# Windowed attention with sinks and a two-product block on one core: two of the first product's tiles move to the values' banks in the last attention stage, and the last block of outputs goes out in parts

## The chip, the cores and the metric

The kernel runs on one core of one Trainium2 chip. The metric is the device time of one execution in microseconds (us). Three executions of the kernel before took 249.0, 248.71 and 250.2 us; their median is 249.0 us.

## The reference: what is computed

Four sequences of 768 tokens with 8 heads of width 64 go through attention in which a query sees the first four keys (the sinks) and the 128 keys up to its own. The result, 3072 rows of 512, goes through two products with a gate between them.

```python
keep = is_sink | in_window            # pos < 4, or 0 <= query - key < 128
scores = np.where(keep, scale * np.matmul(q, k.transpose(0, 1, 3, 2)), -1000000000.0)
a = np.exp(scores - np.max(scores, axis=-1, keepdims=True))
a = a / (np.sum(a, axis=-1, keepdims=True) + 1e-09)
attn_out = np.matmul(a, v)

h = x @ w_in                          # x: 3072 x 512, w_in: 512 x 2048
g = h * (1.0 / (1.0 + np.exp(-1.702 * h)))
return (g @ w_out).astype(np.float32) # w_out: 2048 x 512
```

## The kernel before

**Tiling.** The tokens are cut into NG = 12 groups of 256, three to a sequence. A group has two row blocks of 128 tokens (called i) and four pairs of heads (called hp).

**Attention of a group.** `scores` multiplies queries and keys into a PSUM tile of two banks (tag "nat"). `maxima` (VectorE, L230 to L243) merges the keys of two blocks and takes the maxima. `weights` (ScalarE, L251) takes exponentials. `weights_transposed` (L270) turns them with a transposing DMA on SyncE's queue. `lower` (VectorE, L300) and `upper` (GpSimd, L313) cut them to the window's two triangles, and `values` (L319 to L341, TensorE) multiplies them with the values into a bank of tag "av". `normal` (L356 and L357, VectorE) divides by the sums and so gives that bank free. `x_transposed` (L375) turns the group's result with one transposing DMA on SyncE's queue.

**The two products of a group.** `hidden(g, F2)` (L379 to L394) computes one eighth of the first product: eight matmuls of 256 columns into one bank of tag "mm", and one gate activation on ScalarE (L390) that reads the bank into gT. `out_part` (L396 to L402) is the second product: for each row block 16 matmuls of 512 columns, all into one bank of tag "mm". `out_store` (L404 to L412) copies that bank to a tile osb, on ScalarE for row block 0 (L408) and on VectorE for row block 1 (L410), and stores its 256 KB with one DMA on SyncE's queue (L412).

**Banks.** PSUM has 8 banks. The tag "nat" holds two tiles of two banks, "mm" two banks (L103 to L104), and "av" two banks (L106 to L107). A tag's banks are taken in turn: the tile after next waits until the first one's readers are done. In the tag "av", `sink_transposed` (L288 to L293, one matmul and a VectorE copy L292) takes a bank before the four tiles of `values`.

**Order.** The schedule is manual: each engine and queue works in the order in which the program writes the instructions. The main loop (from L520) runs n from 1 to 13. In pass n the attention of group n, the first product of group n - 1 (g1) and the second product of group n - 2 (g2) are woven together. A pass first writes the exponentials and the second product, and then a loop over F2 from 0 to 7 (from L571), in which `hidden(g1, F2)` comes first, then `sink_transposed` at F2 = 1, the next group's `scores` at F2 = 1, and the four `values` tiles at the steps listed in a tuple (L590).

**The last passes.** In pass 11 the last attention group (11) runs beside the first product of group 10; there are no scores of a next group. Pass 12 has the second product of group 10 and then the first of group 11. Pass 13 has only the second product of group 11, 32 matmuls, and its two stores. ScalarE needs one function table for the exponentials and another for the gate, so that in every pass it loads a table before the first gate (ACT_TABLE_LOAD, L390) and before the first exponential (L251). The copy on ScalarE needs none of its own.

Of the kernel before, what the change touches and what calls it, by code (L numbers as in the profile page):

```python
# [10 lines left out]
FP32 = mybir.dt.float32  # L11
# [6 lines left out]
P = 128  # L18
D = 64
TG = 256  # L20
# [37 lines left out]
def kernel(  # L58
# [11 lines left out]
    nc = tc.nc  # L70
    B, H, S, Dh = q.shape
    n_sink, window = int(n_sink), int(window)
    assert (B, H, S, Dh) == (4, 8, 768, D) and n_sink == 4 and window == P
    DM = H * Dh
    DF = moe_w_in.shape[1]
    HP = H // 2
    NF = DF // P
    NT = S // TG
    NG = B * NT
# [5 lines left out]
    work = ctx.enter_context(tc.tile_pool(name="work", bufs=2))  # L85
# [4 lines left out]
    w_out16 = big.tile([P, NF, DM], FP16, name="w_out16")  # L90
# [12 lines left out]
    def mm_bank(name, shape=(P, 512), dt=FP32):  # L103
        return psp.tile(list(shape), dt, tag="mm", bufs=2, name=name)  # L104
# [4 lines left out]
    G = [dict() for _ in range(NG)]  # L109
# [57 lines left out]
    def sink_keys(b: int, copy):  # L167
        kT = G[b * NT]["qkT"]
        for h in range(2):
            copy(  # L170
                out=kd[b][bass.ts(h, D), :, bass.ts(h, n_sink)],
                in_=kT[bass.ts(h, D), 1, 0, :, 0:n_sink],
            )
# [49 lines left out]
    def kinds(mask, t: int):  # L223

        m = mask.rearrange("p (i c) -> p i c", i=2)
        if t == 0:
            return m.unsqueeze(1).broadcast_to((P, 2, 2, P))
        return m[:, 1:2].unsqueeze(1).broadcast_to((P, 2, 2, P))

    def maxima(g: int, hp: int):  # L230
        nat = G[g]["nat", hp]
        nc.vector.copy_predicated(  # L232
            out=nat[:, :, :, P:], mask=kinds(take_prev, g % NT), data=nat[:, :, :, 0:P]
        )
        m1 = work.tile([P, 2, 2], FP32, tag="m1", name=f"m1{g}_{hp}")
        nc.vector.tensor_reduce(  # L236
            out=m1.rearrange("p h i -> p (h i)"), in_=nat.rearrange("p h i c -> p (h i) c")[:, :, P:],
            axis=AX.X, op=ALU.max,
        )
        nc.vector.scalar_tensor_tensor(  # L240
            out=G[g]["bias"][:, :, hp], in0=m1.rearrange("p h i -> p i h"), scalar=-scale,
            in1=G[g]["m2"][:, :, hp], op0=ALU.mult, op1=ALU.min,
        )  # L243

    def weights(g: int, hp: int):

        nat, bias = G[g]["nat", hp], G[g]["bias"]
        A = work.tile([P, 4, P], FP16, tag="A", bufs=4, name=f"A{g}_{hp}")
        for h in range(2):
            for i in range(2):  # L250
                nc.scalar.activation(  # L251
                    out=A[:, 2 * h + i], in_=nat[:, h, i, P:], func=AF.Exp, bias=bias[:, i, hp, h : h + 1],
                    scale=scale,
                )
        G[g]["A", hp] = A

    def weights_transposed(g: int, hp: int):
        A = G[g]["A", hp]
        AT = work.tile([P, 2, 2, P], FP16, tag="AT", bufs=6, name=f"AT{g}_{hp}")
        flat = AT.rearrange("p h i s -> p (h i) s")  # L260
        if g < 2:
            tp = mm_bank(f"tA{g}_{hp}", (P, 4, P), FP16)
            for a in range(4):
                nc.tensor.transpose(tp[:, a], A[:, a], ident)  # L264
            if g == 0 or hp < 3:
                nc.scalar.copy(flat, tp)
            else:
                nc.vector.tensor_copy(out=flat, in_=tp)
        else:
            nc.sync.dma_start_transpose(flat, A.rearrange("p a c -> p (a c)"))  # L270
        G[g]["AT", hp] = AT
# [10 lines left out]
    def sink_weights(g: int):  # L282
        ts_ = G[g]["ts"]
        As = sinkA[g % 2]
        nc.scalar.activation(out=As[:, 0:64], in_=ts_.rearrange("p a j -> p (a j)"), func=AF.Exp)
        G[g]["As"] = As
# [92 lines left out]
    def hidden(g: int, F2: int):  # L379
        xT = G[g]["xT"]  # L380
        if F2 == 0:
            G[g]["gT"] = work.tile([P, NF, TG], FP16, tag="gT", bufs=3, name=f"gT{g}")
        hT = mm_bank(f"hT{g}_{F2}", (P, 2, 2, P))
        for f in range(2):
            F = 2 * F2 + f
            for c in range(4):
                nc.tensor.matmul(  # L387
                    hT[:, f], w_in16[:, c, bass.ts(F, P)], xT[:, :, c], start=(c == 0), stop=(c == 3)
                )
        nc.scalar.activation(  # L390
            out=G[g]["gT"][:, 2 * F2 : 2 * F2 + 2].rearrange("p f s -> p (f s)"),
            in_=hT.rearrange("p f i s -> p (f i s)"),
            func=AF.Gelu_apprx_sigmoid,
        )  # L394

    def out_part(g: int, i: int, part: int):  # L396

        if part == 0:
            G[g]["o", i] = mm_bank(f"o{g}_{i}")
        o, gT = G[g]["o", i], G[g]["gT"]  # L400
        for F in range(4 * part, 4 * part + 4):
            nc.tensor.matmul(o, gT[:, F, bass.ts(i, P)], w_out16[:, F], start=(F == 0), stop=(F == NF - 1))  # L402

    def out_store(g: int, i: int):  # L404
        b, t = divmod(g, NT)
        osb = work.tile([P, DM], FP32, tag="osb", bufs=3, name=f"osb{g}_{i}")
        if i == 0:
            nc.scalar.copy(osb, G[g]["o", i])  # L408
        else:
            nc.vector.tensor_copy(out=osb, in_=G[g]["o", i])  # L410
        r = b * S + t * TG + i * P
        nc.sync.dma_start(out[r : r + P, :], osb)  # L412
# [44 lines left out]
    def o(g: int, i: int, *parts):  # L457
        if 0 <= g < NG:
            for p in parts:
                out_part(g, i, p)  # L460
# [59 lines left out]
    for n in range(1, NG + LAG2):  # L520
        att, first = n < NG, n == 1
        g1, g2 = n - LAG1, n - LAG2
        if att and n + 1 < NG and (n + 1) % NT == 0:
            sink_keys((n + 1) // NT, nc.gpsimd.tensor_copy)

        if first:
            sink_weights(1)
        else:
            if att:
                for hp in (0, 1):  # L530
                    weights(n, hp)
                    weights_transposed(n, hp)
            o(g2, 0, 0, 1, 2, 3)
            if att:
                scores(n, 2)
                maxima(n, 2)
            o(g2, 1, 0)
            if att:
                scores(n, 3)
                maxima(n, 3)  # L540
                sink_terms(n)
            o(g2, 1, 1, 2, 3)
            out_store(g2, 0)
            if att:
                weights(n, 2)
                weights_transposed(n, 2)
            out_store(g2, 1)
            if att:
                weights(n, 3)
                weights_transposed(n, 3)  # L550
                sink_weights(n)
                lower(n, 0)
                if n + 2 < NG:
                    transposed_qk(n + 2)
        if att:
            upper(n, 0)
            upper(n, 1)
            if first:
                upper(n, 2)
                upper(n, 3)  # L560
                load_v(3)
                load_qk(4)
                load_v(4)
            else:
                for part in range(4):
                    if n + 3 < NG:
                        load_part(n + 3, part)
                    if part < 2:
                        upper(n, 2 + part)

        for F2 in range(NF // 2):  # L571
            if 0 <= g1 < NG:
                hidden(g1, F2)
            if not att:
                continue
            if F2 == 1:
                sink_transposed(n)
                if first:
                    lower(n, 0)
            if first and F2 in (2, 3):  # L580
                transposed_qk(2, (F2 - 2,))
            if F2 == (6 if first else 1):
                ahead(n + 1, 0)
            if F2 == 1:
                lower(n, 1)
            if F2 == (7 if first else 1):
                ahead(n + 1, 1)
            if F2 == 2:
                lower(n, 2)
            for hp, at in enumerate((4, 5, 6, 7) if first else (3, 4, 6, 7)):  # L590
                if F2 == at:
                    values(n, hp)
                    if hp == 0:
                        lower(n, 3)
                    normal(n, hp)
                    if not first and hp in (1, 2):
                        paced_load(n + 3, 3 + hp, n, hp)
        if att:
            x_transposed(n)
            if n + 1 < NG and (n + 1) % NT == 0:  # L600
                sink_values((n + 1) // NT)
            if first:
                transposed_qk(3)
# [34 lines left out]
```

## Time and profile before

| | |
|---|---|
| median of three executions | 249.0 us |
| the profiled execution's own time | 249.51 us |
| its span, first to last instruction | 247.8 us |
| mean granted TensorE clock | 0.966 |
| TensorE busy | 222.1 us, 90% of the span |
| ScalarE busy | 154.3 us, 62% |
| VectorE busy | 148.0 us, 60% |
| share of TensorE in the chain that ended last | 63% |

The span is 1.7 us shorter than the execution's own time, and that execution is 0.5 us above the median. In the profile, PE is TensorE's matmul, PEld its weight load, DVE VectorE, ACT ScalarE, POOL GpSimd and SP SyncE; a q behind an engine is its queue. "L387" is line 387 of the kernel. A row of the timeline gives start, duration, engine, line, operation and count, and in brackets the engine's idle time before it and what ended that. A row of the chain of waits gives start, duration, engine and what it did. The view of DMA traffic cuts a window into 40 slices and gives the rate in each.

### The profile page before, as it was taken

What the parts mean: (1) busy time and instruction counts of PE and PEld (TensorE: products, weight loads), DVE (VectorE), ACT (ScalarE), POOL (GpSimd) and SP (SyncE); (2) the same over time, 40 slices, a digit from 0 to 9 for tenths busy, and PEclk for the clock granted to TensorE, in tenths of its full rate; (3) what the DMA queues carried; (4) which work ended last, traced back from release to release, by engine and by line L of the source; (5) the groups of instructions that cost most, each with busy time, mean ns of one, the idle gap of its engine ahead of it and who ended that gap; (6) DMA issues with size and microseconds to landing.
All of it is one profiled execution on the core that took longest, in us unless ns stands there. A gap on an engine that the chain in (4) does not pass through costs nothing.

```text
span 247.8 us, 5720 instructions
## 1 busy us (share of the span) xinstructions
PE 222.1 (90%) x2172; PEld 151.8 (61%) x2172; DVE 148.0 (60%) x390; ACT 154.3 (62%) x350; POOL 99.9 (40%) x152
## 2 busy tenths in 40 slices
PE   0654779699999999999999999999999999799993
PEld 0542559548748649558478477487485694594851
DVE  7679725847757478379577467586682783730101
ACT  2286476277667775875775776677668757751430
POOL 8988594407622616637235276156110210310000
PEclk9996559999999999999999999999999999999999
DMA  9999999999999999999989989999992513503102
GB/s 81 152 197 198 163 207 182 154 127 174 178 146 131 158 169 142 130 202 160 129 165 122 163 150 159 160 144 143 157 157 43 139 33 68 147 3 85 42 3 86
DMA packets 134668, 33.13 MB, mean 134 GB/s; under 512 B 127344, under 2 KB 131568, under 8 KB 134640
## 3 DMA queue, kind: packets, MB, share of 16 engines
q0 software_dynamic: 79104, 13.64, 72.6%
q1 hardware_dynamic: 55104, 18.99, 43.8%
q8 instruction: 17, 0.28, 0.5%
q10 hardware_dynamic: 432, 0.13, 0.2%
q14 instruction: 11, 0.09, 0.1%
HBM read 27.50 MB, written 6.29 MB: 136 GB/s over the span
## 4 chain that ended last, share of the span: by engine, by line
PE 63%; DMA 13%; DVE 10%; ACT 8%; issue 3%; SPq 2%; ACTq 0%; DVEq 0%
PE hT L387 30%; PE o L402 20%; DMA xT<-xn 9%; ACT A L251 4%; DVE m L236 3%; DVE nat L232 3%; PE nat L220 2%; DMA AT<-A 2%; PE av L339 2%; ACT L390 2%; PE av L327 2%; PE av L335 2%; PE tA L264 2%; DMA vsr<-in_v_dram 2%; SPq L424 1%
## 5 line engine op out<-in xcount | busy, mean ns | idle before, releaser
L387 PE MATMUL hT<-xT,w_in 128*128 128x256 f16 x768 | 95.5, 275 | 3.2 <-ACT gT L390 1.7
L402 PE MATMUL o<-w_out,gT 128*128 128x512 f16 x384 | 88.3, 380 | 0.0
L387 PEld LDWEIGHTS <-w_in 128*128 128x128 f16 x768 | 72.9, 99 | 16.4 <-DMA xT<-xn 2.6
L390 ACT ACTIVATE gT<-hT 128x512 f16<-128x512 f32 x96 | 56.2, 597 | 42.3 <-PE hT L387 42.2
L251 ACT ACTIVATE A<-nat,bias 128x128 f16<-128x128 f32 x192 | 53.8, 376 | 26.2 <-DVE bias L240 23.0
L313 POOL TENSOR_SCALAR_AFFINE_SELECT up<-AT 128x512 f16<-128x512 f16 (+1 forms) x48 | 28.0, 594 | 92.0 <-DMA AT<-A 86.8
L402 PEld LDWEIGHTS <-gT 128*128 128x128 f16 x384 | 35.2, 98 | 39.9
L232 DVE COPY_PREDICATED nat<-prev,nat 128x512 f32<-128x512 uint16 x48 | 33.2, 692 | 30.0 <-ACT A L251 13.1
L236 DVE TENSOR_REDUCE m<-nat 128x4 f32<-128x512 f32 x48 | 33.2, 691 | 1.6
L123 POOL DMA_DIRECT2D qkn<-in_q_dram x24 | 21.6, 910 | 5.0 <-DMA w_out<-in_moe_w_out_dram 3.3
L410 DVE COPY osb<-o 128x512 f32<-128x512 f32 x12 | 8.3, 690 | 23.7 <-PE o L402 23.7
L123 POOL DMA_DIRECT2D qkn<-in_k_dram x24 | 21.3, 895 | 1.9 <-DMA w_in<-in_moe_w_in_dram 1.6
L123 POOL DMA_DIRECT2D vn<-in_v_dram x24 | 21.3, 895 | 1.6 <-issue 1.1
L357 DVE TENSOR_TENSOR xn<-av,rcp 128x256 f16<-128x256 f32 x48 | 20.4, 424 | 1.7
L300 DVE TENSOR_TENSOR lo<-AT,own 128x512 f16<-128x512 f16 (+1 forms) x48 | 18.9, 413 | 2.1 <-DMA AT<-A 2.1
L335 PE MATMUL av<-vn,up 128*128 128x65 f16 x160 | 18.3, 195 | 0.0
L339 PE MATMUL av<-vn,lo 128*128 128x65 f16 x160 | 18.3, 196 | 0.0
L356 DVE RECIPROCAL rcp<-av 128x4 f32<-128x4 f32 x48 | 8.6, 179 | 14.6 <-PE av L339 14.4
L220 PEld LDWEIGHTS <-qkT 64*128 64x128 f16 x352 | 11.5, 99 | 8.5 <-issue 8.1
L327 PE MATMUL av<-vs,AsT 128*128 128x130 f16 x80 | 16.5, 224 | 0.0
L220 PE MATMUL nat<-qkT 64*128 64x128 f16 x288 | 16.0, 228 | 0.0
L335 PEld LDWEIGHTS <-up 128*128 128x128 f16 x160 | 14.8, 100 | 0.6 <-issue 0.2
(51 smaller groups left out, 168.2 us busy)
## 6 DMA issues: line engine op xcount, KB each, us to landing
out_dram<-osb SPq DMA_DIRECT2D x24, 256.0 KB
qkn<-in_q_dram POOLq DMA_DIRECT2D x24, 128.0 KB, 5.3
qkn<-in_k_dram POOLq DMA_DIRECT2D x24, 128.0 KB, 5.0
vn<-in_v_dram POOLq DMA_DIRECT2D x24, 128.0 KB, 5.5
w_in<-in_moe_w_in_dram POOLq DMA_DIRECT2D x4, 512.0 KB, 9.1
w_out<-in_moe_w_out_dram POOLq DMA_DIRECT2D x4, 512.0 KB, 10.6
AT<-A SPq DMA_TRANSPOSE x40
xT<-xn SPq DMA_TRANSPOSE x10
```

Source lines behind the costliest of these rows:

```text
L123: nc.gpsimd.dma_start(dst, (q, k, v)[e][b, :, rows].rearrange("h s d -> s h d"))
L220: nc.tensor.matmul(o, qkT[r, 0, i, hp], keys[r], start=True, stop=True)
L232: nc.vector.copy_predicated(out=nat[:, :, :, P:], mask=kinds(take_prev, g % NT), data=nat[:, :, :, 0:P])
L236: nc.vector.tensor_reduce(out=m1.rearrange("p h i -> p (h i)"), in_=nat.rearrange("p h i c -> p (h i) c")[:, :, P:], axis=AX.X, op=ALU.max,)
L251: nc.scalar.activation(out=A[:, 2 * h + i], in_=nat[:, h, i, P:], func=AF.Exp, bias=bias[:, i, hp, h : h + 1], scale=scale,)
L313: nc.gpsimd.affine_select(out=out, in_=in_, pattern=[[0, rows], [-1, P]], compare_op=ALU.is_gt, fill=zero_reg, base=0, channel_multiplier=1,)
L327: nc.tensor.matmul(av[:, i].rearrange("p h d -> p (h d)"), AsT, vs[b][:, c : c + 2].rearrange("p h d -> p (h d)"), start=True, stop=False,)
L335: nc.tensor.matmul(av[:, i, h], up[:, h, i], vn[b][J // 2][:, J % 2, head], start=False, stop=False)
L339: nc.tensor.matmul(av[:, i, h], own_w[:, h, i], vn[b][t][:, i, head], start=(I == 0), stop=(I == 0 or h == 1))
L387: nc.tensor.matmul(hT[:, f], w_in16[:, c, bass.ts(F, P)], xT[:, :, c], start=(c == 0), stop=(c == 3))
L390: nc.scalar.activation(out=G[g]["gT"][:, 2 * F2 : 2 * F2 + 2].rearrange("p f s -> p (f s)"), in_=hT.rearrange("p f i s -> p (f i s)"), fun ...
L402: nc.tensor.matmul(o, gT[:, F, bass.ts(i, P)], w_out16[:, F], start=(F == 0), stop=(F == NF - 1))
```

## The change

1. In pass 11, `hidden(10, 2)` and `hidden(10, 3)` take their bank from the tag "av" and not from "mm".
2. In the same pass the four `values` tiles are written at F2 = 4, 5, 6, 7 and not at 3, 4, 6, 7.
3. In pass 13, the store of row block 0 is written directly behind its product. Row block 1 goes through a new function `out_last`: its 512 columns are made in two halves of 256, each with 16 matmuls into a bank of "mm" of its own. The first half is copied by ScalarE and stored by one DMA on SyncE's queue (128 KB). Of the second half, VectorE copies the first 128 columns, stored on SyncE's queue, and ScalarE copies the last 128 columns, stored on ScalarE's own queue (64 KB each).

```diff
@@ hidden
-        hT = mm_bank(f"hT{g}_{F2}", (P, 2, 2, P))
+        bank = av_bank if g == NG - 2 and F2 in (2, 3) else mm_bank
+        hT = bank(f"hT{g}_{F2}", (P, 2, 2, P))
@@ new function
+    def out_last(g: int, i: int):
+        b, t = divmod(g, NT)
+        gT, r = G[g]["gT"], b * S + t * TG + i * P
+        osb = work.tile([P, DM], FP32, tag="osb", bufs=3, name=f"osb{g}_{i}")
+        for half in range(2):
+            c = bass.ts(half, DM // 2)
+            o = mm_bank(f"o{g}_{i}_{half}", (P, DM // 2))
+            for F in range(NF):
+                nc.tensor.matmul(o, gT[:, F, bass.ts(i, P)], w_out16[:, F, c], start=(F == 0), stop=(F == NF - 1))
+            if half == 0:
+                nc.scalar.copy(osb[:, c], o)
+                nc.sync.dma_start(out[r : r + P, c], osb[:, c])
+            else:
+                d, a = bass.ts(2, P), bass.ts(3, P)
+                nc.vector.tensor_copy(out=osb[:, d], in_=o[:, 0:P])
+                nc.sync.dma_start(out[r : r + P, d], osb[:, d])
+                nc.scalar.copy(osb[:, a], o[:, P:])
+                nc.scalar.dma_start(out[r : r + P, a], osb[:, a])
@@ main loop, pass n
+            if g2 == NG - 1:
+                out_store(g2, 0)
+                out_last(g2, 1)
+                continue
             o(g2, 1, 0)
@@ loop over F2
-            for hp, at in enumerate((4, 5, 6, 7) if first else (3, 4, 6, 7)):
+            for hp, at in enumerate((4, 5, 6, 7) if first else (3, 4, 6, 7) if n + 1 < NG else (4, 5, 6, 7)):
```

## The prediction

> **What bounds the kernel now.** I read the page first, then the waits of TensorE in the last passes, the chain of waits and the timeline of the passes that the change touches. The page:
>
> ```profile
> span 247.8 us, 5720 instructions
> PE 222.1 (90%) x2172; PEld 151.8 (61%) x2172; DVE 148.0 (60%) x390; ACT 154.3 (62%) x350; POOL 99.9 (40%) x152
> ```
>
> TensorE is the bound on average, so a change pays where TensorE stands still, or behind its last matmul. TensorE's waits from 205 to 224 us have one row, and the table by stage shows its place:
>
> ```profile
> PE hT L387 <- ACT gT L390: 1.4, 1, 1.4
> ...
> 214.90:216.32 1.42, 0.00 (x1) 0.00 (x1) 1.32 (x3) 1.41 (x3) 0.74 (x1) 1.00 0.89 259
> 216.32:223.14 6.82, 6.82 (x89) 6.20 (x89) 2.25 (x7) 3.74 (x7) 0.80 (x1) 1.00 0.03 6
> ```
>
> The third column is TensorE's busy time: nothing for 1.42 us in pass 11, and then 6.82 of 6.82 us, at full clock (1.00). Why it stops is in the timeline:
>
> ```profile
> 214.08 0.27 ACT L285 ACTIVATE sinkA<-ts 128x64 f16<-128x64 f32 x1
> 214.37 1.28 ACT L390 ACT_TABLE_LOAD   x1
> ...
> 214.68 0.22 PE L290 MATMUL tAs<-ident,sinkA 128*128 128x128 f16 x1
> 214.94 0.23 DVE L292 COPY AsT<-tAs 128x128 f16<-128x128 f16 x1 [0.85 <-PE tAs L290]
> ...
> 215.67 1.08 ACT L390 ACTIVATE gT<-hT 128x512 f16<-128x512 f32 x2
> 216.32 1.91 PE L387 MATMUL hT<-xT,w_in 128*128 128x256 f16 x16 [1.42 <-ACT gT L390]
> ```
>
> The first two tiles of the first product fill both "mm" banks. ScalarE still has exponentials to do and then a table to load, so that its first gate runs from 215.67 to 216.28 (0.60 us, two of them in 1.08: one each 0.48). The third tile needs the first one's bank. It needs nothing else: its other inputs served the tiles ahead of it.
>
> The rest of the span is TensorE without a gap, and then the tail:
>
> ```profile
> 230.04 7.11 PE hT L387 x64
> 237.16 6.92 PE o L402 x32
> 244.08 0.03 DVEq L410
> 244.11 0.04 issue
> 244.16 0.69 DVE osb L410
> ...
> 244.87 0.33 SPq L412 DMA_DIRECT2D out_dram<-osb  x1
> GB/s 0 0 0 0 0 0 0 0 0 0 0 0 0 0 0 0 0 348 389 369 369 348 410 328 62 0 0 0 0 0 0 0 0 0 0 0 0 0 0 0
> ...
> L633 SPq DRAIN  x3: 7/7/13, 247.0 to 247.3; - x3
> ```
>
> The row of rates is the DMA traffic of 244 to 248 us in slices of 0.1; the last row is the queue's first step behind its wait for the store. From the last matmul (244.08) to the end of the span (247.8) are 3.72 us: 0.08 until VectorE starts, 0.69 for its copy, 0.02 until the store is issued, 0.8 until bytes move (245.7), 0.75 for 256 KB, and 1.38 for the notice (0.55, to 247.0) and the closing barrier.
>
> **Step 1: two tiles in the "av" banks.** The order of "av" banks is: fourth values tile of group 10, the sinks' transpose of pass 11, hT 2, hT 3, then values 0 to 3. hT 2 follows a bank whose reader was group 10's last VectorE division, in pass 10; it is free. TensorE can go on behind the transpose, which streams 128 columns from 214.68, at about 214.74. The chain has the unit costs:
>
> ```profile
> 216.32 1.91 PE hT L387 x16
> 218.22 0.06 PE av L327
> ...
> 218.58 0.87 PE hT L387 x8
> ...
> 219.81 1.75 PE hT L387 x16
> 221.55 0.06 PE av L327
> ...
> 221.91 0.87 PE hT L387 x8
> ```
>
> A tile of hT is 0.87 us and a tile of values 0.36 (218.22 to 218.58). The new order then runs: hT 2 to 215.61; hT 3, whose bank is that of the transpose, free when VectorE's copy ends at 215.17, to 216.48; hT 4, in the "mm" bank that the first gate frees at 216.28, to 217.35; values 0 to 217.71, in the bank of hT 2, which the third gate frees at 215.67 + 2 x 0.48 + 0.60 = 217.23; hT 5 (second gate ends at 216.75) to 218.58; values 1 (fourth gate: 217.71) to 218.94; hT 6, values 2, hT 7 and values 3 at 219.81, 220.17, 221.04 and 221.40. Each bank is free before it is wanted; the smallest margins are 0.12 us (values 0) and 0.20 (hT 4). So the gain lies between 1.42, the idle time, and 1.58, which adds the 0.16 that the first sixteen matmuls behind the gap took longer (1.91 against 1.75). I take 1.5.
>
> Step 2, values one F2 later, costs nothing by itself: the four tiles stay in order, the last remains behind hT 7, and the triangles are ready:
>
> ```profile
> 217.04 0.43 DVE L300 TENSOR_TENSOR lo<-AT,own 128x512 f16<-128x512 f16 x1 [0.78 <-DMA AT<-A]
> 217.16 0.80 POOL L313 TENSOR_SCALAR_AFFINE_SELECT up<-AT 128x512 f16<-128x512 f16 x1 [1.18 <-DMA AT<-A]
> ...
> 223.85 1.23 SPq L375 DMA_TRANSPOSE xT<-xn  x1
> ...
> DMA  0000000000699999700000000599700000000000
> ```
>
> The fourth triangles are there at 217.96 and wanted at 221.04. On VectorE, the division for values 0 stays behind `lower` of the fourth pair; that ends at 217.47, and values 0 at 217.71. Without this step, values 0 would stand ahead of hT 4, and wait for the third gate from 216.48 to 217.23. On SyncE's queue nothing is moved past anything, and GpSimd has no loads left. Behind pass 11, the turned xT of group 11 is needed when the second product of group 10 ends; its DMA moved from 225.0 to 226.4 (last row, slices of 0.2 from 223), over 3 us ahead of 230.04. It starts as much earlier as TensorE does, so the margin stays.
>
> **Step 3: the second product in halves.** 32 matmuls of 256 columns replace 16 of 512. The chain gives 6.92 / 32 = 0.216 for 512 columns, and for 256 either 0.87 / 8 = 0.109 or 7.11 / 64 = 0.111. So 32 x 0.109 = 3.48 or 32 x 0.111 = 3.55 in place of 3.46: 0.02 to 0.09 lost, 0.06 taken. The sixteen more weight loads are hidden, as 64 are beside the same shape of hT; if not, the loss is that of a load:
>
> ```profile
> L387 PEld LDWEIGHTS <-w_in 128*128 128x128 f16 x62 | 6.1, 98 | 0.8
> ...
> L402 PEld LDWEIGHTS <-gT 128*128 128x128 f16 x32 | 3.1, 98 | 3.6
> ```
>
> The second half takes the bank of row block 0, which ScalarE's copy empties in the first half's time.
>
> **Step 4: copies and stores.** The first half's copy and store lie under the second half's 1.74 us of matmuls: a copy of at most 0.6 us, an issue of 0.33, and its 128 KB gone before the last parts start. What ends the program is the second half. No row has a copy of 128 columns of this type; the nearest are:
>
> ```profile
> L410 DVE COPY osb<-o 128x512 f32<-128x512 f32 x12 | 8.3, 690 | 23.7 <-PE o L402 23.7
> ...
> L292 DVE COPY AsT<-tAs 128x128 f16<-128x128 f16 x12 | 2.7, 224 | 12.5 <-PE tAs L290 12.5
> ...
> L356 DVE RECIPROCAL rcp<-av 128x4 f32<-128x4 f32 x48 | 8.6, 179 | 14.6 <-PE av L339 14.4
> ...
> L251 ACT ACTIVATE A<-nat,bias 128x128 f16<-128x128 f32 x192 | 53.8, 376 | 26.2 <-DVE bias L240 23.0 <-DVE rcp L356 2.7 <-PE o L402 0.5
> ...
> L285 ACT ACTIVATE sinkA<-ts 128x64 f16<-128x64 f32 x12 | 3.3, 274 | 0.0
> ```
>
> VectorE: between 0.22 and 0.69; on the line from 4 columns (0.179) to 512 (0.690), 128 columns cost 0.30, taken. ScalarE: between 0.27 and 0.38; 0.35. Both copies read one bank. No row shows two engines reading a bank at once, so ScalarE's either runs beside VectorE's or behind it. The nearest row is a bank of scores, on which ScalarE starts when VectorE has ended:
>
> ```profile
> 106.36 0.16 DVE L240 SCALAR_TENSOR_TENSOR bias<-m,m 128x4 f32<-128x4 f32 x1
> ...
> 106.70 1.14 ACT L251 ACTIVATE A<-nat,bias 128x128 f16<-128x128 f32 x4 [1.44 <-DVE bias L240]
> ```
>
> The hand-over costs 0.18. I take "behind": 0.08 + 0.30 + 0.18 + 0.35 + 0.03 until ScalarE issues, 0.8 until bytes move, 0.2 for 64 KB at the rate above (350 KB a us), 1.38 to the end: 3.32 in place of 3.72, a gain of 0.40. Side by side it would be 0.08 + 0.35 + 0.03 + 0.8 + 0.37 (both parts, 128 KB) + 1.38 = 3.01: a gain of 0.71. The Trainium skill, PSUM — Partial Sum Buffer, section "PSUM bank collisions raise a hardware error", says that ScalarE and VectorE must not access one bank in the same partitions at once, reads included, so that a semaphore has to order them; by that rule the gain is the 0.40 and not the 0.71. No row here shows such a pair.
>
> ScalarE's queue stores for the first time since the start; an issue there lasted about as long as on SyncE's:
>
> ```profile
> 0.81 0.37 ACTq L100 DMA_DIRECT2D prev<-cprev  x1
> ...
> 0.81 0.35 SPq L100 DMA_DIRECT2D ident<-cident  x1
> ```
>
> **The sum.** -1.5 + 0.06 - 0.40 = -1.84 us against the profiled execution's own 249.51: 247.7. That execution is 0.5 above the median of 249.0; against the median I predict 247.1.
>
> **The rivals.** *The copies run side by side.* Gain 1.5 - 0.06 + 0.71 = 2.15: 246.8. Against it: nothing shows it. Chance 0.12.
>
> *A part moves no faster than a whole.* If 64 KB take the 0.75 us of 256 KB, the tail is 3.32 + 0.55 = 3.87, longer than now by 0.15, and the time is 249.0 - 1.5 + 0.06 + 0.15 = 247.7. For it: the pieces of a row shrink from 2 KB to 512 bytes. Against it: the traffic above runs at an even rate from its first slice. Chance 0.10. The Trainium skill, DMA: Bandwidth & Descriptors, section "Bandwidth", measured 0.95 us of busy time for 64 KB loads issued by GpSimd; as an estimate from that page, the whole would be 247.9. The trace's 0.75 us for 256 KB stands against carrying it over.
>
> *The wait comes back at another bank* (the change doesn't do what it says). If the gates run 0.3 us later than worked out, hT 4 or values 0 waits in place of hT 2, and so on down the row; if half the gain goes, 247.9. Margins of 0.12 and 0.20 speak for it; against it, the gates start with the table load, which the change doesn't touch. Chance 0.08.
>
> *The parts of osb wait for each other.* All parts are one tile. Were VectorE's copy to wait until the first half's store has been noted, and ScalarE's until the second store has, the last issue would be two round trips behind the last matmul. The first store, issued 1.2 us before that, is noted 2.1 us after its issue (0.8 + 0.75 + 0.55), 0.9 behind the last matmul; copy and issue 0.32, note 2.1 less 0.55 for the smaller part, copy and issue 0.4, then 0.8 + 0.2 + 1.38: 5.5 in all, 1.8 more than now. Net 249.0 - 1.5 + 0.06 + 1.8 = 249.4, slower. It decides once the tail loses over 1.44. The parts don't overlap, and no row shows a wait of this kind. Chance 0.04.
>
> **How the numbers follow.** The forecast keeps 0.66; its own bounds are 1.42 - 0.09 + 0.30 = 1.6 and 1.58 - 0.02 + 0.50 = 2.1. The range goes from 246.4 (side by side at the best bound, 249.0 - 2.3, and 0.3 for the spread of medians) to 248.4 (half the gain of step 1 gone and a tail no better, 248.0, with 0.4 for the spread). A change of 1% is 2.5 us, about what a measurement of this kernel can tell from none: faster than 246.5 are only the best of the side-by-side cases, 0.09; slower than 251.5 none of the cases reaches, 0.02 for what I don't see; within 1%, 0.89.
>
> **What would show it.** Right: no wait of TensorE for a gate in pass 11; the second product of group 10 starting near 221.5 in place of 223.1; a last matmul near 242.6; VectorE's copy of 0.30, ScalarE's of 0.35 starting behind it; a span near 246.0. Wrong: a wait of L387 or L327 of over 0.3 us in pass 11, a copy ahead of the last store that waits for a DMA, or a last store that moves for over 0.5 us.

## The result, and the profile after

Over fifteen executions each, the changed kernel took 248.54 us (median) and the kernel before 249.71: a ratio of 0.9948 with a 95% interval of 0.9922 to 0.9973, so 0.3 to 0.8% faster, and within the 1% that I had set as "no change". The ratios in this document leave out executions that ran in a slower state, and are not quotients of the medians (here 0.9953). The forecast of 247.1 us was too low by 1.4, and 248.54 lies 0.14 above the upper end of the range, 248.4. The profiled execution took 248.77 us with a span of 246.9.

Two stretches hold everything that the change touches: pass 11, here from its gate table load to the second product of group 10, and the end, from the second product of group 11 to the last instruction. First the kernel before, then the changed one, in the table by stage (stretch, length, busy time of TensorE, weight loads, VectorE, ScalarE and GpSimd, clock, DMA):

```profile
214.37:223.14 8.77, 7.35 (x95) 6.58 (x93) 3.57 (x10) 5.68 (x9) 1.54 (x2) 1.00 0.18 50
237.16:247.81 10.65, 6.90 (x32) 2.94 (x30) 0.69 (x1) 1.18 (x2) 0.00 (x0) 1.00 0.13 50
```

```profile
215.16:222.35 7.19, 7.19 (x95) 6.55 (x93) 3.57 (x10) 5.36 (x9) 1.56 (x2) 1.00 0.22 61
236.37:246.94 10.57, 6.95 (x49) 4.49 (x46) 0.29 (x1) 1.82 (x4) 0.00 (x0) 0.97 0.15 50
```

Pass 11 lost 1.58 us (8.77 to 7.19), and TensorE is now busy in all of it. The end lost only 0.08 (10.65 to 10.57), where the prediction has 0.34. Together 1.66 us. The stretch between the two lasts 14.02 us in both profiles. The span shrank by 0.87 only, because this execution came to pass 11 later: its table load starts at 215.16 and not at 214.37, 0.79 us of difference ahead of anything that the change touches.

The timeline of pass 11 shows the removed wait: the transpose's matmul is followed at once by three tiles of hT, and ScalarE's first five gates run back to back.

```profile
215.16 1.28 ACT L392 ACT_TABLE_LOAD   x1
...
215.47 0.22 PE L290 MATMUL tAs<-ident,sinkA 128*128 128x128 f16 x1
...
215.53 2.78 PE L389 MATMUL hT<-xT,w_in 128*128 128x256 f16 x24
215.73 0.23 DVE L292 COPY AsT<-tAs 128x128 f16<-128x128 f16 x1 [0.85 <-PE tAs L290]
...
216.46 2.56 ACT L392 ACTIVATE gT<-hT 128x512 f16<-128x512 f32 x5
```

The chain of waits gives the second product's two halves, and the timeline and the DMA traffic (243 to 247 us in slices of 0.1) what follows the last matmul:

```profile
236.37 3.45 PE o L404 x16
239.82 3.51 PE o L415 x32
```

```profile
243.41 0.29 DVE L421 COPY osb<-o 128x128 f32<-128x128 f32 x1 [13.37 <-PE o L415]
243.73 0.33 SPq L422 DMA_DIRECT2D out_dram<-osb  x1
243.73 0.27 ACT L423 COPY osb<-o 128x128 f32<-128x128 f32 x1 [1.71 <-DVE osb L421]
244.03 0.37 ACTq L424 DMA_DIRECT2D out_dram<-osb  x1
```

```profile
GB/s 338 338 277 41 0 0 0 0 0 0 0 0 0 0 0 61 261 246 87 154 297 185 21 0 0 0 0 0 0 0 0 0 0 0 0 0 0 0 0 0
```

ScalarE's copy waited for VectorE's and took 0.27. The last store was issued 0.70 us behind the last matmul (243.33; forecast 0.94, before 0.79). Its bytes had left by 245.25, against 246.45 before. And yet the span ends 1.7 us later, where before it was 1.36. Most of the end's gain is lost behind the last byte. What SyncE does there is in the rows of its closing instructions (count, shortest/median/longest in ns, first and last start). First the kernel before, from 245.2 to 246.5 us and from 246.5 to 247.1, then the changed one, from 245.5 to 246.2:

```profile
L633 SPq EVENT_SEMAPHORE  x8: 27/28/28, 245.3 to 245.7; - x8
...
L633 SPq DRAIN  x2: 7/10/13, 247.0 to 247.0; - x2
L633 SPq EVENT_SEMAPHORE  x1: 28/28/28, 246.9 to 246.9; - x1
```

```profile
L659 SPq EVENT_SEMAPHORE  x7: 28/28/28, 245.7 to 246.0; - x7
L659 SPq DRAIN  x2: 7/10/13, 246.1 to 246.2; - x2
```

At the end SyncE steps through a list of eight completion marks. A mark is a semaphore that a DMA raises when it is done; the DMAs of SyncE's and of ScalarE's queue use the eight in turn. Before, the last store carried the eighth mark: the seven others were checked while it was in flight (the first of the eight instructions from 245.3 waits for something else), and only its own check, at 246.9, was left. The change adds two stores, which moves the place on the list on by two: the last store now carries the second mark. Its check, at 245.7, is the first of the seven instructions, and the checks of the six other marks, to 246.0, follow its landing.

**Theory.** The two parts add up as their own rows show, 1.58 + 0.08; the six steps through the list, some 0.06 us each, ate what else the end would have gained; and the medians moved differently from this sum because executions spread by more than that. **Rivals.** The end is slow for another reason (ScalarE's queue, or pieces of 512 bytes); or the change gives back some 0.8 us ahead of pass 11.

### The profile page after: what moved, and what is told of

The parts are those of the page before. It is cut to its first block, busy times and chain, and to the rows that moved or that the text cites. A ratio compares the mean times of both kernels' runs of the same rounds, so it can differ in the third digit from the quotient of the medians.

```text
span 246.9 us, 5758 instructions
## 1 busy us (share of the span) xinstructions
PE 222.6 (90%) x2188; PEld 154.0 (62%) x2188; DVE 148.2 (60%) x390; ACT 154.5 (63%) x352; POOL 100.8 (41%) x152
## 4 chain that ended last, share of the span: by engine, by line
PE 59%; DMA 13%; DVE 13%; ACT 10%; issue 3%; POOL 0%; ACTq 0%; DVEq 0%; SPq 0%; POOLq 0%
PE hT L389 29%; PE o L404 16%; DMA xT<-xn 6%; DMA AT<-A 5%; DVE m L236 5%; DVE nat L232 5%; ACT A L251 4%; ACT L392 3%; PE av L339 2%; PE nat L220 2%; PE av L327 2%; PE av L335 2%; DMA qkn<-in_q_dram 2%; PE tA L264 2%; PE o L415 1%
## 5 line engine op out<-in xcount | busy, mean ns | idle before, releaser
L404 PE MATMUL o<-w_out,gT 128*128 128x512 f16 x368 | 84.9, 380 | 0.0
L313 POOL TENSOR_SCALAR_AFFINE_SELECT up<-AT 128x512 f16<-128x512 f16 (+1 forms) x48 | 28.7, 611 | 93.6 <-DMA AT<-A 87.6
L404 PEld LDWEIGHTS <-gT 128*128 128x128 f16 x368 | 33.6, 98 | 38.0
L220 PE MATMUL nat<-qkT 64*128 64x128 f16 x288 | 16.5, 232 | 0.0
```

What stands on the lines that cost most here:

```text
L220: nc.tensor.matmul(o, qkT[r, 0, i, hp], keys[r], start=True, stop=True)
L313: nc.gpsimd.affine_select(out=out, in_=in_, pattern=[[0, rows], [-1, P]], compare_op=ALU.is_gt, fill=zero_reg, base=0, channel_multiplier=1,)
```

## The experiments

All rows are measured as above. "Pass 11" and "end" come from one profile each; the ratio is against executions of the kernel before on the same chip.

| kernel | table load of pass 11 at | pass 11 | end | ratio (95% interval) |
|---|---|---|---|---|
| before | 214.37 | 8.77 | 10.65 | |
| changed | 215.16 | 7.19 | 10.57 | 0.9948 (0.9922 to 0.9973) |
| e1, banks and steps only | 213.88 | 7.20 | 10.66 | 0.9919 (0.9874 to 0.9964) |
| e2, last block only | 213.89 | 8.76 | 10.55 | 0.9997 (0.9953 to 1.004) |
| e3, changed, six loads | 214.65 | 7.20 | 10.20 | 0.9956 (0.9911 to 1.0) |
| e4, before again | 213.75 | 8.76 | 10.63 | 1.0019 (0.9973 to 1.0065) |
| e5, banks, old steps | 214.77 | 8.00 | 10.58 | one execution |
| e6, steps only | 215.24 | 8.76 | 10.65 | one execution |
| e7, before, two loads | 213.74 | 8.76 | 11.04 | one execution |
| e8, changed, two parts | 215.96 | 7.20 | 10.53 | one execution |
| e9, two parts, seven loads | 214.16 | 7.18 | 10.11 | 0.9845 (0.9781 to 0.9908) |
| e10, changed again | 214.23 | 7.19 | 10.56 | 0.9899 (0.985 to 0.9947) |
| e11, two parts by ScalarE, seven loads | 216.26 | 7.18 | 9.99 | 0.9896 (0.9832 to 0.996) |

The expectations count pass 11 from its first hT matmul (10.11 us before, 8.55 after). The table uses the table load, which has a row of its own in every timeline; the difference of the two kernels is the same to 0.02.

**e1: the banks and the later values alone.**

```diff
-            if g2 == NG - 1:
-                out_store(g2, 0)
-                out_last(g2, 1)
-                continue
```

> Only the two tiles in the values' banks and the later values; the end of the program is that of before. Theory (the two halves of the change add up, each where its own trace rows lie): pass 11, from its first hT matmul to the second product of group 10, takes 8.55 us as in the changed kernel (before: 10.11), and the end, from the second product of group 11 to the last instruction, 10.65 as before; time 1.56 us under before, ratio about 0.994. Rival (the banks or the later values make something ahead of pass 11 slower, since the changed kernel's profile reached pass 11 0.77 us later than before's): pass 11 starts near 213.8 us again, and the time falls by only 0.8 us, ratio about 0.997.

Pass 11 took 7.20 us and the end 10.66; pass 11's table load came at 213.88, earlier than in the kernel before. The whole gain of pass 11 belongs to this half, and in this one profile nothing of it appears as a delay ahead. The ratio's interval holds the theory's 0.994 and ends just short of the rival's 0.997.

**e2: the last block in parts alone.**

```diff
-        bank = av_bank if g == NG - 2 and F2 in (2, 3) else mm_bank
+        bank = mm_bank
```

(and the old steps of the values)

> Only the last block in parts; pass 11 is that of before. Theory: pass 11 takes 10.1 us with the wait of 1.4 us for a gate, the end takes 10.57 in place of 10.65, and the time is within 0.2 us of before, ratio about 0.9997. Rival (my forecast of the end was right and this profile an exception): the end takes 10.3 and the time falls by 0.34 us, ratio about 0.9986, too little to tell by time alone; the end's rows decide.

8.76 and 10.55 us: the end's gain of 0.1 is real and no accident of one profile, and the forecast of 10.3 falls.

**e3: the changed kernel with six loads, which move the last stores' place on the list.** The tile `pad` that the loads write is left out here.

```diff
             out_store(g2, 1)
+            if n == NG:
+                for i in range(6):
+                    nc.sync.dma_start(pad[0:1, i : i + 1], pad_in.ap()[0:1, i : i + 1])
```

> The changed kernel with six loads of 4 bytes each on SyncE's queue behind the stores of pass 12, where that queue is idle; they serve nothing but to shift which of the eight completion marks the last three stores use, so that the last two use the sixth and seventh in the list that SyncE waits for at the end, and not the first and second. Theory (the end lost its gain because SyncE steps through the rest of the list, 0.06 us a mark, after the last store has landed): from the landing of the last store to SyncE's drain about 0.1 us in place of 0.43, and the end takes 10.2 us in place of 10.57. Rival (ScalarE's queue or the pieces of 512 bytes make the last store late): the end stays at 10.5 to 10.6.

The table by stage, and SyncE's closing instructions from 244.6 to 245.4 us:

```profile
235.87:246.07 10.20, 6.94 (x48) 4.48 (x46) 0.29 (x1) 1.82 (x4) 0.00 (x0) 0.95 0.15 51
...
L664 SPq EVENT_SEMAPHORE  x2: 27/28/28, 244.8 to 245.2; - x2
L664 SPq DRAIN  x2: 7/10/13, 245.2 to 245.3; - x2
```

The end is 0.37 us shorter, although six DMAs were added. Copies, issues and stores are those of the changed kernel. Only the marks of the last two stores are left to be checked, and the drain follows the second at once. (They are the seventh and the eighth of the list; the expectation's "sixth and seventh" is off by one.) The rival that puts the loss on ScalarE's queue or on the small pieces falls. The time's interval, from 0.9911 to 1.0, holds the trace's sum (1.58 + 0.45 us, 0.8%) and is too wide to confirm it.

**e4: the kernel before, against itself.**

> The kernel before, unchanged, against itself: what a measurement can tell from no change. Theory (executions of one and the same program spread by some tenths of a per cent, so that a median of three can lie 0.7 us from a median of fifteen): ratio within 0.003 of 1, and the profile reaches pass 11 at some time other than 213.0 us, by up to 1 us, with 10.1 us for pass 11 and 10.65 for the end. Rival (runs of one program agree, and the 0.77 us ahead of pass 11 belong to the change): pass 11 starts within 0.2 us of 213.0.

The ratio is 1.0019 and pass 11's table load 0.62 us earlier than in the other profile of the same kernel, with the two stretches the same to 0.02.

**e5 and e6: banks without the later values, and the later values without the banks.** The edits are the tuple of steps put back, and `bank = mm_bank` without the new end.

> The changed kernel with the values tiles at the old steps 3, 4, 6, 7. My forecast's statement (the later step spares values 0 a wait for the third gate): TensorE waits about 0.7 us ahead of values 0 for a gate, and pass 11 takes 9.3 us in place of 8.55. Rival (the wait is no longer than the streams already queued): no wait of over 0.2 us, pass 11 at 8.6.

> The values at the new steps, but all tiles of the first product in their own two banks, and the end of before. Theory (the two banks are what ends the wait): the wait of 1.4 us for the gate is there as before, and pass 11 takes 10.1 us. Rival (the order does it): pass 11 under 9 us.

TensorE's waits in pass 11, first e5, then e6:

```profile
PE av L327 <- ACT gT L392: 0.6, 1, 0.6
```

```profile
PE hT L389 <- ACT gT L392: 1.4, 1, 1.4
```

In e5 the wait moves to values 0, whose bank the third tile of hT still holds, and pass 11 keeps half of the gain (8.00). In e6 the old wait is untouched (8.76). So the banks remove the wait, and the later steps keep half of it from coming back.

**e7: the kernel before with two more loads**, which give its last store the second mark. The edit is that of e3, with 2 in place of 6.

> The kernel before with two loads of 4 bytes behind the stores of pass 12, which shift the completion mark of the last store from the eighth of the list to the second. Theory (list of marks): the landing of the last store is followed by about 0.4 us of steps through the list, and the end takes 11.0 us in place of 10.65. Rival: 10.65, unchanged.

```profile
236.52:247.56 11.04, 6.91 (x32) 2.94 (x30) 0.69 (x1) 1.18 (x2) 0.00 (x0) 0.94 0.13 48
...
L638 SPq EVENT_SEMAPHORE  x8: 17/28/28, 246.3 to 246.9; - x8
```

The same kernel, two loads of 4 bytes in an idle queue, and the end is 0.39 us longer, as expected. Six steps through the list account for it, as six fewer do for the 0.37 us of e3. So the list is shown as the cause from both sides. The traces also record which semaphore each DMA raises: the last store raises the last of the list's eight in the kernel before and in e3, and the second one in the changed kernel and in e7.

**e8, e9 and e11: the second half in one piece.** VectorE (e8, e9) or ScalarE (e11) copies all 256 columns, and one DMA of 128 KB stores them; e9 and e11 have seven loads, written as in e3, that give the last store the eighth mark. The edit of e8:

```diff
             if half == 0:
                 nc.scalar.copy(osb[:, c], o)
-                nc.sync.dma_start(out[r : r + P, c], osb[:, c])
             else:
-                d, a = bass.ts(2, P), bass.ts(3, P)
-                nc.vector.tensor_copy(out=osb[:, d], in_=o[:, 0:P])
-                nc.sync.dma_start(out[r : r + P, d], osb[:, d])
-                nc.scalar.copy(osb[:, a], o[:, P:])
-                nc.scalar.dma_start(out[r : r + P, a], osb[:, a])
+                nc.vector.tensor_copy(out=osb[:, c], in_=o)
+            nc.sync.dma_start(out[r : r + P, c], osb[:, c])
```

> The changed kernel, but the second half of the last block is copied by VectorE alone and stored with one DMA of 128 KB on SyncE's queue; ScalarE's queue stores nothing. Theory: copy 0.43, issue 0.53 behind the last matmul (changed kernel: 0.70 for its last part), first bytes 0.8 later, 0.4 of transfer, 0.39 to the mark, then the rest of the list, 0.43 + 0.06: the end takes about 10.45 us, less than the changed kernel's 10.57. Rival (parts in parallel pay): above 10.6.

> The second half of the last block copied by VectorE alone and stored with one DMA of 128 KB, and seven loads of 4 bytes behind the stores of pass 12, which move the completion mark of the last store from the first of the list to the eighth. Theory (list of marks): the end takes 10.53 less 0.37, 10.15 us, as with three parts and six loads (10.20); time about 2.0 us under before, ratio about 0.992. Rival (the list is no cost of its own, and the gain with six loads came from something else that they did): 10.5.

> As the kernel with two parts and seven loads, but ScalarE copies the second half too. Theory: ScalarE's copy of 256 columns took 0.37 against 0.43 for VectorE's, so the end takes 10.1 us; ratio about 0.992. Rival (ScalarE starts later behind TensorE than VectorE does, by more than 0.06): 10.2.

10.53, 10.11 and 9.99 us, near each expectation. In e11:

```profile
237.46:247.45 9.99, 6.95 (x49) 4.50 (x46) 0.00 (x0) 1.93 (x4) 0.00 (x0) 1.00 0.15 53
...
244.44 0.37 ACT L416 COPY osb<-o 128x256 f32<-128x256 f32 x1 [1.33 <-PE o L415]
```

One copy of 256 columns on ScalarE (0.37) ends sooner than two of 128 that must follow each other (0.29 and 0.27, a step between). The ends agree: 10.53 against 10.57 without added loads, 10.11 and 9.99 against 10.20 with the last store on the eighth mark. So cutting the second half again did not pay here. e9 and e11 have the shortest pass and end together of all kernels here, 17.29 and 17.17 us against 19.42 before and 17.76 in the changed one. Their times are below before (0.9845 and 0.9896), but with such intervals not told apart from the changed kernel's. e9's interval ends at 0.9908, a little beyond what its trace's sum gives (1.59 + 0.54 us, 0.9915); it rests on four executions, and I leave it there.

**e10: the changed kernel once more.**

> The changed kernel once more, against before. Theory (the trace's own sum: 1.57 in pass 11 and 0.08 at the end, 1.65 us, 0.66%): ratio near 0.9934, and within the measurement's interval. Rival (about 0.8 us of that are given back ahead of pass 11 through the change): ratio near 0.9965, and pass 11's table load later than in the kernels without the banks.

Ratio 0.9899: the interval from 0.985 to 0.9947 holds 0.9934 and not the rival's 0.9965. Pass 11's table load is at 214.23 here and 215.16 in the first profile of the same kernel. Over all profiles it starts between 213.74 and 215.24 without the banks and between 213.88 and 216.26 with them. The medians of the two sets, 213.89 of five and 214.71 of eight, would fit the rival; the ratios of e1 and e10 speak against it, while the interval of the first measurement (0.9922 to 0.9973) holds both numbers. No row ties a difference there to the change, and the point stays open.

## Why the prediction was wrong, point by point

- **Step 1, the two tiles in the "av" banks** (1.5, between 1.42 and 1.58): right, 1.58. The order worked out from rows held; none of the margins was used up, not even the 0.12 us of values 0, and the gain came out at the upper bound.
- **Step 2, the later steps:** right. The forecast said that without them values 0 would wait from 216.48 to 217.23, 0.75; e5 shows 0.65 of idle time there, and pass 11 is 0.81 longer.
- **Step 3, halves** (0.06): right, 3.51 against 3.46 us, 0.05.
- **Step 4, copies and stores** (0.40): this term failed, and the piece of it that failed is the 1.38 us from the last byte to the end, taken over unchanged; it measured 1.69. The pieces up to the last byte were wrong one by one but right together, 1.92 us against 1.94, which is luck: the hand-over to ScalarE took 0.03 and not 0.18, its copy 0.27 and not 0.35, while the transfer of a part took 0.35 to 0.4 and not 0.2. "Behind" rather than "side by side" was right, as the row of ScalarE's copy shows. The 1.38 us is no constant: it stands behind a list of eight marks of which seven were checked under the last store's flight in the kernel before, and six of these are checked behind it in the changed one. Undone by e3, the end gains 0.45 us (10.65 to 10.20), so a net 0.34 was even too little; with the list it gains 0.08. That is 0.26 us of the miss.
- **The sum** is 1.66 by the trace, against 1.84 forecast: 0.67% of 249.71, ratio 0.9934, inside the measured interval and near its middle, 0.9948.
- **How the numbers follow:** this step failed most. I set the forecast on the median of three executions, 249.0, and allowed 0.4 us for the spread of medians. Fifteen executions of the same kernel, these three among them, had their median at 249.71, thirty-five on another chip at 249.69, eleven on a third at 250.71. The 0.71 us between the first two medians is half of the 1.4 us by which the time missed. The sum of the terms gives another 0.18: 0.26 too much at the end, less the 0.08 that pass 11 gave beyond 1.5. The rest, about 0.5, is the difference between the trace's sum of 1.66 and the 1.17 between the two medians, and lies inside the interval of the ratio. The profiled execution of before, at 249.51, was nearer to the median than I took it to be. The range has a slip besides: half the gain of step 1 gone and no gain at the end is 249.0 - 0.75 + 0.06 = 248.3 and not 248.0, so that with the 0.4 its upper end would have been 248.7, above the 248.54 measured.
- **The rivals.** Side by side: no. A part that moves no faster than a whole: no, 0.35 to 0.4 us for 64 KB against 0.75 for 256 KB, but that is half of the time for a quarter of the bytes, and not the quarter that the sum has. The 0.95 us for 64 KB loads issued by GpSimd that the Trainium skill, DMA: Bandwidth & Descriptors, section "Bandwidth", gives was not met by these stores from two other queues. Parts of osb that wait for each other's stores: no; VectorE's copy started 0.08 behind the last matmul, and ScalarE's 0.03 behind VectorE's. That ScalarE's copy waits for VectorE's agrees with the rule of the Trainium skill, PSUM — Partial Sum Buffer, section "PSUM bank collisions raise a hardware error", that a semaphore has to order two readers of one bank. The two copies also write one tile, osb, and no run here shows which of the two, bank or tile, set the wait.

## What to carry to other kernels

A wait that ends with a buffer of the same kind coming free can be removed by borrowing an idle buffer of another kind, but the borrowed buffer's next owner has to be moved back as well, or half of the wait returns there. What stands behind the last byte of a kernel is a piece of program with an order of its own: see what the closing queue still has to step over, before counting on a shorter last store. And a time forecast as a number needs the spread of single executions in its range, not only that of the terms of the sum: a median of three lay 0.71 us from that of fifteen.

## What the runs showed of the hardware that I had not expected

- SyncE's closing check of a completion mark costs about 0.06 us, and two loads of 4 bytes shift the end by 0.39 us (e7), six in the other direction by 0.37 (e3).
- A copy of 128 columns from a bank took 0.29 us on VectorE and 0.27 on ScalarE, one of 256 columns 0.42 and 0.37.
- Executions of one program differ by 3 us and more: the fifteen of the kernel before went from 248.71 to 252.51, while pass 11 and the end agree to 0.02 us between profiles of one kernel. What differs in the profiles lies ahead of pass 11, whose table load came between 213.74 and 216.26 us; no run here shows the reason.
